# Loading k and q with three tokens side by side, and turning them two heads at a time, in a chunk-selected attention with a gated feed-forward

## The chip, the core and the metric

The kernel runs on one core of a Trainium2 chip. A core has TensorE (PE, matrix products out of the on-chip memory SBUF into the banks of PSUM), VectorE (DVE), ScalarE (ACT), GpSimd (POOL) and SyncE (SP, which issues transfers), each with its own instruction stream, and 16 DMA engines. The metric is the device time of one execution in microseconds, as the median of several runs.

## What is computed

Attention over 4 batches, 8 heads, 768 tokens and a head size of 64. Keys are cut into chunks of 32 tokens; every query keeps the six chunks with the highest upper bound of its score, and attends to the tokens of these that are not behind it. The heads side by side are the input of a feed-forward layer with a root-mean-square norm and a gate.

```python
k_min, k_max = k_chunks.min(3), k_chunks.max(3)
ub = sum(maximum(q * k_min, q * k_max), -1)          # per query and chunk, causal
top_chunks = argsort(ub)[..., -6:]
scores = q @ k.T / sqrt(64), kept where the chunk is chosen and not later
attn_out = softmax(scores) @ v
x = attn_out as (3072, 512)
xn = x / sqrt(mean(x * x) + 1e-6) * rms_g
out = (silu(xn @ w_gate) * (xn @ w_val)) @ w_out     # 512 -> 1536 -> 512
```

## The kernel before

The 32 heads are worked on as 16 pairs of heads, four pairs to a batch. Every piece of work is a step, created by a call of `add` with its name, and a long string, `PROGRAM`, writes out the order of all steps: a word such as `P155:5` means step 155, on TensorE (P), with buffer slot 5; A is ScalarE, D VectorE, G GpSimd, S SyncE. Each engine carries out its words in that order. Numbers that `add` is given as durations and loads served to find an order; they change nothing in what an engine executes.

The steps of one pair, in `prep`:

- `kload`, `qload` (lines 494 to 511): k or q of two heads come from memory as fp32 into a tile `knat` or `qnat` of 128 partitions x 6 blocks x 2 heads x 64. Token 128 t + p of a head lies in partition p, block t, so one contiguous run is one token of one head, 64 words or 256 bytes. Two transfers per tensor, one per head; for pair 0 in halves.
- `kT`, `qT` (lines 517 to 522): three blocks are turned into one PSUM bank, by three transpositions on TensorE of 128 tokens x 128 (two heads of 64) against an fp32 identity. A tensor of a pair takes two such banks. For 16 pairs these are 32 banks of k and 32 of q.
- `kE`, `qE` (lines 530 to 533): ScalarE or VectorE copies the bank, 128 x 384 words, to `kt` or `qt`.
- `kmx`, `kmn`, `dif`: minimum, maximum and difference of each chunk from `kt`. `kC`: GpSimd casts `kt` to bf16 for the scores. For q, the first three pairs (`QM = 3`) are cast from `qt` in the same way (`qC`); later pairs are cast from `qnat` as it was loaded (`qN`, then turned by a DMA, `qX`).
- `relu`, `ub`: the upper bounds are a sum of two fp32 products, of the chunk minima with q and of the differences with relu(q). For the first six pairs `bounds` at line 731 writes 2 (products) x 3 (thirds of the queries) x 2 (heads) products at line 737, for two pairs together `duo` writes 2 x 4 x 2 at line 795. Each has 64 rows and 32 columns of weights and is put at its own place of the array by `tile_position`.
- `up`, `ubm`, `max`, `sel`: transposing back, the causal mask, the six best, the choice.

Then `scores` (`sc` line 882, `exp` line 899, `av` line 918), `norm` and `ffn` (`gate` line 1051, `tanh`, `tg`, `val` line 1072, `hh`, `po` line 1092). The weights of the feed-forward are loaded in halves from GpSimd's queue (`wg`, `wv`, `wo`).

`busy` steps (line 339) are fillers on TensorE: a product of zeros with 512 columns, used by nothing. 48 may be placed; the order has 26 of them.

Of the kernel before, what the change touches and what calls it, by code (L numbers as in the profile page):

```python
# [28 lines left out]
    "S83:0 S88:1 S89 S82 D3 G0 D56 D55 D53 D54 D60 G63 A2 G65 P4:0 D59 P5:1 G66 P6:2 D58 P7:3 D57 G67 P8:4 S154:2 "  # L29
    "P9:5 G68 P86:6 S159:3 P10:7 G72 A87:0 P11:0 A69 D97:0 P92:1 D96:0 P12:2 G64 S335:4 G73 P84:3 D93:1 P90:4 A85 "  # L30
    "P13:5 P14:7 A91 P15:6 D95 P16:0 A99:0 P17:2 G101 D94 S222:5 P157:1 P155:5 D98 G62 A158:2 D103:3 P18:3 G61 "
    "P19:7 P20:4 S71 D156 P104:6,0 G102 D1 D52 D165:1 G168:1 P160:2 S330:6 A106:0 P162:3 D164:1 G74 A105 P21:1 "
    "A161:4 P107:7 A163 G167 P336:4 S70 D108:0 P338:5 A171:5 P22:0 G166 D109:2 P23:6 P24:1 A100 D110 S541:0 "
    "P172:2,3 A337:6 D112:0 A339 D111 P225:7 A173:0 D174 P113:0 G346:3 A226:1 S227:1 P175:6 A114 P223:1 D176:1 "
    "P25:4 P26:5 D177:3 P331:2 P333:3 D178 A224 G115:0 S404:2 P119:7 D332:2 A334 P147:6 A179:1 P135:4 D340:4 "
    "A148:0 G170 P128:5 P116:0 A136:1 D180 S399:3 P544:1 A117:2 D341:2 P150:3 P125:2 A545:0 P181:6 P141:4 A151:3 "
    "D232:5 A126:4 P138:0 G342 G236:2 P347:1,3 A120:5 D182 A129:6 G169 P228:2 A139:7 P230:7 S546:5 G183:1 D348:0 "
    "A349 P542:5 D229:5 A231 P350:6 D233:3 A142:8 P190:0 G345:0 P118:1 P121 A239:6 P144:3 P149:2 D351:2 P152 "
    "P184:7 G234 G235 A191:9 D352:6 P240:4,6 D543 A145:2 G238 D353 A185:5 P215:0 P122:5 G251:2 A241:0 D242 P143 "
    "A216:0 P146 P131:3 P243:7 A354 P405:4 A123:3 G237 D244:0 P209:6 P140 P137 A132:8 P218:0 D245:7 P193:7 A210:2 "  # L40
    "G358:3 P407:5 D406:3 A219:7 P203:3 A194:1 D246 P133 P124 P187:6 A408 D248:0 G247 P127 A204:8 P196:0 D153:0 "
    "P402:4 A188:3 P199:7 P217:5 P249:3 D355 A197:4 P130 P212:2 D250 S356:0 P211 A403:4 P195:6 G556:1 P206:0 "
    "A200:0 A213:6 P186 P400:4 G555:1 D134 A207:2 P264:7 P201 S357 P286:3 P214 P277:2 A265:1 G554 D401 P189 "
    "P258:0 P252:1 A278:5 D409:0 G343 P274:7 A259:0 S475:6 P261:4 A253:6 P205 D552:0 P192 G344 P198 P255:2 A275:3 "
    "P271:0 G415:1 D202 A256:8 S470:1 P267:1 P279:7 P220 P208 A287:9 A268:4 P266:2 D551:1 P283:6 A272:5 P288 "
    "P362:3 P257 P276 A262:7 P280:1 S75 D221 P269 P254 P369:0 P260 A281:2 P359:4 G412:2 D410:1 A370:1 P263 P282 "
    "A284:9 P273 P366:5 G76 D270 A363:8 P285 A360:3 P389:1 G77 P371:0 P364:6 P386:3 D329 A367:4 P361 P373:2 "
    "A390:6 G411 D365 G553 P368 P395:4 G78 A387:0 P471:5 D372 P416:7,1 D472:6 A1248:2,0 D1246:1 A1247:2 P379:6 "
    "P478:3 D418:0 A396:7 P547:0 D1249:3 D417 P27:5 A374:2 G1250:4 P397:1 D548:5 P392:4 P476:7 A380:5 P382:5 "
    "P473:2 D1251:0 A383:9 P391 P388 P376:0 A393:1 D1254:1 P375:6 P384 P1252:5 A479:2 P394 D1257:2 P381 A477 "  # L50
    "P1255:4 P419:3 A377:8 D398 G486:0 P1258:7 A1253:0 P378 D1259 P549:0 A1256 D385 P28:1 P29:5 A474 D420:1 "
    "P1260:7 A1336:5,0 D421:7 G413 P1280:1 A1335:1 D480:6 P1268:4 A1337:2 G414:0 D422 A1261:0 P1285:6 D1338:0 "
    "D423 A1281:1 D424 G1339:1 P1270:5 D1262:2 A1286:3 S426 D1282:4 P1275:2 A1271:5 D1346:3 P1263:3 A1276:6 S425 "
    "D1272:7 P1265:7 D1277:0 P1305:1 D1343:0 A1266:1 S559:0 P1288:5 D550 D1264:0 P1344:2 G557:3 P1315:0 D1287:5 "
    "A1345 S564:4 D1267:6 P439:3 A1316:2 P449:6 D1289:1 P445:2 P1300:7 A450:3 D1269:2 P1295:5 G427:0 A440:4 "
    "D481:2 A1301:3 P1283:6 A446:7 D1317:1 G79 A1296:5 P457:4 D1302:6 P560:3 A458:6 P436:2 G482 D1297:2 P1347:0 "
    "G81 A561:1 P562:7 D1348 P565:4 A563 D1284:3 P428:5 P463:3 A437:0 D1340:1 P432:0 G572:0 P487:7,6 A429:2 "
    "D570:3 A464:9 P1273:2 G451 A489:0 D488 A566:4 P1341:5 G485:0 P567:3 A1306:3 D1342 P459:6 A433:1 P490:7 "
    "D1274:4 G430 P1364:4 D569:2 G80 P466:5 P1349:0 A467:5 D491:0 P465 P442:2 D571 D568 P1399:5 A443:8 D1307:5 "
    "P460:7 P452 D575:2 A1400:4 P1278:3 A461:6 D1401:7 P577:2,1 A1350:3 D492:3 A1365:4 D493 G494 P453:7 P1308:5 "  # L60
    "A582:0 D578 A454:9 P1298:1 D1309:5 G455 P583:2 G484:2 D1299:6 P579:7 P462 D1366:5 P456 P1389:5 G434 D581:2 "
    "G483 D580:1 P468 P1392:1 D585 A1390:2 D584 D469:1 G573 P1310:4 D586:4 P1318:7 D592:5 D495 P1402:2 D1351:4 "
    "S496 P1374:6 D1279:7 D1391:3 P438:0 P1354:3 S497 D1393:8 P1303:5 D1403:9 A1355:0 P1367:1 A1375:2 D587 "
    "A1311:3 S700:3 D1319:10 P1290:2 G588 D1356:7 G498:1 P1379:7 D1312:1 A1291:0 P1293:3 D1368:11 A1380:3 G576:2 "
    "D1304:12 P524:4 P1325:1 D1292:5 A525:3 G574:0 D1294:13 P503:5 P444 D1381:6 P510:2 G526 P431 P447 P528:4 D593 "
    "A511:6 P1313:3 D589 A529:9 G594 P435 D1376:0 P703:7 S591 A504:5 P701:2 D1314:14 P1394:4 D595 D702:0 P537:6 "
    "P507:5 S590 P520:3 A538:0 D704 A1395:5 P1326 A521:8 D1396:3 P513:2 G522 S597 P1359:6 A514:2 P539:7 P441 "
    "P499:3 P1327 D448 A500:7 S596 A1360:2 P534:4 G501 P598:2 D1328:0 P1352:0 A535:1 G505 S682:1 A508:0 P516:3 "
    "P523 P506:1 D1353:15 P1384:4 A599:4 D1361:1 A517:8 P530 P536 P531:5 S705:5 D710:7 A1385:5 P512 P509 P665:0 "
    "A532:5 G714:2 P515 P678:2 P527 D1386:4 P672:3 A666:9 P518 P675:6 G558:3 D711:1 S841:2 P533 A673:1 P606:5 "  # L70
    "P502 P669:4 A679:6 P644:0 A676:0 D540 P661:3 G667 P1320:2 A607:2 G713 S823:0 D519 A662:3 P685:6 A670:8 "
    "P674:7 G663 P680 P623:5 D686:5 P657:3 P668 P683:1 G715:1 S687:6 A658:5 A645:7 P671 P1321 D684 A624:1 G646 "
    "D693:2 P648:4 G625 P651:6 S1329 P640:3 A649:6 P654:0 D692:0 P612:1 A641:9 P1322 A613:8 G642 P677 P706:5 "
    "D1323:1 G696:0 A655:0 P650:4 P842:3 S828:4 D707:3 A652:6 P647 P614:1 G712 P609:2 G600 P656 A843:4 P664 "
    "P626:0 P643 A610:7 P653 D681 G694 P633:5 S1324 P708:6 A634:8 P659 P615:3 P601 P826:2 A709 P611 P824:7 S846:3 "
    "D827:2 P602:5 G716:6 P630:6 A825 D660 P1369:2 A616:0 A603:3 D834:0 P1357:7 A631:1 S987:1 P608 A1370:2 P619:3 "
    "D833:6 P690:4 G604 A620:9 P636:5 P617 P635 G699:0 P688:6 D1371:5 A691:1 P605 P627:3 A689 P632 S982:5 D618 "
    "P844:2 G858:1 A628:6 P1362:4 D1358:16 A845 P629 A698:0 P831:6 D852:3 G621 P1382:1 A637:5 G854:1 P622 P638 "
    "P718:3,7 D639 G695 D1363:17 A1425:1,0 G697:0 P1377:2 A1426:1 D719:0 G717:2 P849:5 A1424:2 P720:0 D850:5 "
    "P1404:4 A1510:2,0 G835 D1378:18 P847:3 D721:0 A1405:2 P829:5 D832:1 A1511:1 P1330:2 D1427:3 D1406:7 G1428:4 "  # L80
    "A848 D722:1 P1407:6 A830 A723 D1429:2 P1387:4 D1433:0 P724:3 S1430:1 P1331 D1408:19 D1383:20 P1397:0 S1434 "
    "D1431:3 P1372:5 D1398:21 P1409:7 S1432 D1388:22 D1373:23 P1419:6 D726 S1105:0 D733:5 P1414:1 D734 D725 P1420 "
    "G735 D736 P1415 D851:7 S737 P1455:0 D727:0 D728 P1440:4 S738 A1456:1 D730 P1332 A729 D853 A839:0 S731 "
    "P1460:5 A1441:0 A1512:2 P1410 A1461:2 S732 A1333:2 P1445:3 D1462:7 D1442:6 P983:2 P1411 D1513:6 S969:2 "
    "A984:3 G1514:1 A1446:3 P789:5 P785:4 D1412:0 G856:1 P1421 A790:4 S1334 D1447:4 A786:7 G838:0 S1413 P792:2 "
    "D857:6 P760:7 A1422:1 P781:5 S1110:6 G855 P747:3 A793:2 P1450:4 D1457:5 A748:0 D1517:1 P753:6 A782:8 P1470:2 "
    "S964:3 A761:3 P739:0 D1519:2 P1435:3 A1471:2 G762 A740:1 D1472:0 P1108:5 S1123:4 A1436:3 P743:7 G783 P1438:0 "
    "D1109:4 A1451:1 D1437:2 A754:6 P1416 S1520 A744:9 P755:2 P1106:5 G745 D1417:2 P816:3 G741 P746 S1128:0 "
    "P795:6 D1452:3 A817:5 P791:7 P1443:1 G840:3 D1439:24 A1107 P742 P819:4 P750:3 D1444:25 S1423 P1465:0 A820:6 "
    "G787 A796:9 D1115:3 S1518 P859:5,4 A751:4 A1466:1 D1515:0 S1418 D1467:2 P967:1 S1516 A864:0 D860 P756:6 "  # L90
# [1073 lines left out]
```

## Time and profile before

| | |
|---|---|
| median of three runs | 311.89 us (311.79 to 312.59) |
| the profiled execution | 312.63 us |
| its span, first to last instruction | 310.9 us |
| TensorE busy | 300.8 us (97%) |
| VectorE, ScalarE, GpSimd busy | 232.2, 182.2, 119.5 us |
| read from memory, written | 28.57 MB, 6.29 MB |
| packets of the hardware queue q1 | 83152 |

The profile is of one execution. PE stands for products on TensorE and PEld for its weight loads, which overlap them. The ends of products are modelled, so spans of PE overlap, and what a product costs in a row of others is better read from the chain of waits, where pieces stand end to end. In groups of instructions the columns are line, engine, operation, out<-in, shape and count, then busy us and the mean of one in ns, then the idle time of the engine just before them and what ended it. "128*128" behind an operation on TensorE is the size of the array's tile in rows*columns.

### The profile page before, as it was taken

How to read it: one execution, taken by the hardware profiler on the slowest of the kernel's cores; microseconds unless marked ns; L12 is line 12 of the kernel's file. 1: busy time of each engine (PE TensorE's matmuls, PEld its weight loads, DVE VectorE, ACT ScalarE, POOL GpSimd, SP SyncE). 2: the span in 40 equal slices, each digit the busy share in tenths (PEclk: the TensorE clock that was granted, in tenths of full speed). 3: DMA queues.
4: the chain of work that ended last, by engine and by line, in shares of the span. 5: the costliest groups of instructions: out<-in, count | busy, mean ns of one | idle time of the engine just before them, and what ended most of it. 6: DMA issues, size and time to landing. Idle time of an engine off the chain costs nothing.

```text
span 310.9 us, 7415 instructions
## 1 busy us (share of the span) xinstructions
PE 300.8 (97%) x2764; PEld 190.4 (61%) x2782; DVE 232.2 (75%) x651; ACT 182.2 (59%) x405; POOL 119.5 (38%) x176
## 2 busy tenths in 40 slices
PE   7989998999999999999999999999999999999995
PEld 3657875666667764667776456666665455565542
DVE  5888988998977887789987897875743764477621
ACT  5789987672588763866997336667872303433110
POOL 8588856654547840632775104514030110000000
PEclk9999999999999999999999999999999999999999
DMA  9999999999999997996237136533000055200013
GB/s 172 221 170 175 121 209 209 158 168 150 154 176 206 201 163 145 231 163 165 55 26 50 33 74 178 53 74 29 3 0 2 34 86 186 102 2 0 0 70 136
DMA packets 113300, 35.35 MB, mean 114 GB/s; under 512 B 106224, under 2 KB 110064, under 8 KB 113264
## 3 DMA queue, kind: packets, MB, share of 16 engines
q1 hardware_dynamic: 83152, 26.62, 43.0%
q0 software_dynamic: 28512, 7.87, 25.4%
q10 hardware_dynamic: 1600, 0.39, 0.6%
q8 instruction: 22, 0.36, 0.5%
q14 instruction: 14, 0.11, 0.1%
HBM read 28.57 MB, written 6.29 MB: 112 GB/s over the span
## 4 chain that ended last, share of the span: by engine, by line
PE 87%; DMA 8%; POOL 2%; ACT 1%; issue 1%; ACTq 0%; SPq 0%; POOLq 0%
PE vp L1072 20%; PE po L1092 20%; PE gp L1051 19%; PE sc L882 10%; PE av L918 6%; DMA wg<-in_moe_w_gate_dram 5%; PE pq L520 3%; PE pk L520 3%; PE ub L795 2%; DMA knat<-in_k_dram 2%; PE ub L737 1%; DMA qnat<-in_q_dram 1%; POOL ke L294 1%; PE up L817 1%; PE busy L339 1%; POOL rt L638 1%
## 5 line engine op out<-in xcount | busy, mean ns | idle before, releaser
L899 ACT ACTIVATE pt<-sc 128x512 bf16<-128x512 f32 (+1 forms) x192 | 94.0, 556 | 21.2 <-PE sc L882 18.4
L1058 ACT ACTIVATE sg<-gp 128x384 bf16<-128x384 f32 x96 | 45.7, 495 | 72.2 <-PE gp L1051 62.6
L1072 PE MATMUL vp<-xT,wv 128*128 128x384 bf16 x384 | 74.4, 326 | 1.6 <-DMA wv<-in_moe_w_val_dram 1.5
L1051 PE MATMUL gp<-xT,wg 128*128 128x384 bf16 x384 | 74.2, 326 | 0.1
L1092 PE MATMUL po<-wo,hh 128*128 128x512 bf16 x271 | 66.8, 379 | 0.7
L1064 DVE SCALAR_TENSOR_TENSOR tg<-sg,gp 128x384 bf16<-128x384 bf16 x96 | 51.9, 549 | 20.6 <-ACT sg L1058 19.2
L1080 DVE TENSOR_TENSOR hh<-vp,tg 128x384 bf16<-128x384 f32 x96 | 51.5, 552 | 18.5 <-PE vp L1072 17.7
L882 PE MATMUL sc<-qs,ke 128*128 128x128 bf16 (+4 forms) x420 | 59.3, 251 | 0.0
L1072 PEld LDWEIGHTS <-wv 128*128 128x128 bf16 x384 | 35.8, 98 | 26.4 <-DMA wv<-in_moe_w_val_dram 1.8
L1051 PEld LDWEIGHTS <-wg 128*128 128x128 bf16 x384 | 35.7, 98 | 22.5 <-DMA wg<-in_moe_w_gate_dram 0.5
L1092 PEld LDWEIGHTS <-hh 128*128 128x128 bf16 x288 | 27.5, 98 | 27.5
L918 PEld LDWEIGHTS <-pt 128*128 128x128 bf16 x672 | 34.8, 98 | 11.1 <-POOL pt L905 0.3
L918 PE MATMUL av<-vx,pt 128*128 128x65 bf16 x672 | 41.2, 193 | 0.1
L905 POOL TENSOR_SCALAR_AFFINE_SELECT pt<-pt 128x512 bf16<-128x512 bf16 (+1 forms) x48 | 24.5, 522 | 38.5 <-ACT pt L899 38.1
L882 PEld LDWEIGHTS <-ke 89*128 89x128 bf16 (+1 forms) x420 | 31.0, 97 | 10.0 <-issue 1.4
L294 POOL CAST ke<-kt 64x768 bf16<-64x768 f32 x30 | 25.3, 846 | 7.3 <-PE sc L882 2.8
L987 POOL TENSOR_TENSOR ri<-ms,mhalf 128x3 f32<-128x3 f32 x8 | 7.2, 904 | 33.6 <-DVE ms L979 33.5
L995 DVE SCALAR_TENSOR_TENSOR xs<-xb,ri,gains 128x512 bf16<-128x512 bf16 x24 | 17.2, 751 | 3.1 <-POOL ri L987 2.9
L939 DVE TENSOR_TENSOR xb<-av,rden 128x384 bf16<-128x384 f32 (+1 forms) x34 | 18.2, 534 | 1.2
L520 PE MATMUL pk<-ident_f,knat 128*128 128x128 f32 x96 | 16.0, 282 | 1.7 <-DMA knat<-in_k_dram 1.7
L476 POOL DMA_DIRECT2D vx<-in_v_dram x16 | 17.3, 1079 | 0.1
L653 DVE MAX8 m<-ubm 128x8 f32<-128x8 f32 (+4 forms) x192 | 16.8, 160 | 0.2
(91 smaller groups left out, 300.6 us busy)
## 6 DMA issues: line engine op xcount, KB each, us to landing
out_dram<-osb SPq DMA_DIRECT2D x24, 256.0 KB, 2.3
knat<-in_k_dram SPq DMA_DIRECT2D x30, 192.0 KB, 4.4
qnat<-in_q_dram SPq DMA_DIRECT2D x30, 192.0 KB, 5.1
vx<-in_v_dram POOLq DMA_DIRECT2D x16, 192.0 KB, 5.9
wg<-in_moe_w_gate_dram POOLq DMA_DIRECT2D x2, 768.0 KB, 11.7
wv<-in_moe_w_val_dram POOLq DMA_DIRECT2D x2, 768.0 KB, 10.6
wo<-in_moe_w_out_dram POOLq DMA_DIRECT2D x2, 768.0 KB, 11.8
qs<-qn SPq DMA_TRANSPOSE x26, 2.8
```

What stands on the lines that cost most here:

```text
L294: engine[e].tensor_copy(out_, in_)
L520: nc.tensor.transpose(t[:, j * P:(j + 1) * P], nat[w].tile[:, j0 + j].rearrange("p h d -> p (h d)"), ident_f[:])
L882: nc.tensor.matmul(t[:, x:x + m, :].rearrange("p a b -> p (a b)"), ke[kk, kb * P:(kb + 1) * P], qs[kk, q0 * P:(q0 + m) * P], start=not tri ...
L899: nc.scalar.activation(out=t[:, 0:nn, :], in_=sc.tile[:, 0:nn, :], func=ACT.Exp, scale=SCALE)
L905: nc.gpsimd.affine_select(out=pt.tile[:, 0:nd, :], in_=pt.tile[:, 0:nd, :], compare_op=ALU.is_ge, fill=0.0, base=0, pattern=[[0, nd], [1, ...
L918: nc.tensor.matmul(av.tile[:, qi - i0, :], pt.tile[:, x, :], VX[c.v.slot][:, hl * NT + kb, :], start=(begin and m == 0), stop=(left[0] == ...
L1051: nc.tensor.matmul(t[:], wg[:, g, hs], XT[b].tile[:, g, cols], start=(g == 0), stop=(g == NP - 1))
L1058: nc.scalar.activation(out=t[:], in_=gp.tile[:], func=ACT.Tanh, scale=0.5)
L1064: nc.vector.scalar_tensor_tensor(out=t[:], in0=sg.tile[:], scalar=1.0, in1=gp.tile[:], op0=ALU.add, op1=ALU.mult)
L1072: nc.tensor.matmul(t[:], wv[:, g, hs], XT[b].tile[:, g, cols], start=(g == 0), stop=(g == NP - 1))
L1080: nc.vector.tensor_tensor(out=t[:], in0=vp.tile[:], in1=tg.tile[:], op=ALU.mult)
L1092: nc.tensor.matmul(po.tile[:], hhs[ht].tile[:, th * P:(th + 1) * P], wo[:, ht, :], start=(ht == 0), stop=(ht == NHT - 1))
```

## The change

**Load.** For k of all 16 pairs (`K3 = 16`) and q of the first three (`Q3 = 3`), three consecutive tokens of a head lie side by side in a partition: token 384 g + 3 p + s is in partition p, group g, place s. One contiguous run is 768 bytes. The bytes and the number of transfers stay.

**Turning.** The two heads of a token block no longer lie side by side, so a block is turned by two products with the fp32 identity, each with 64 columns of weights, head h into rows 64 h to 64 h + 63 of the bank, by `tile_position=(0, 64 h)`. A bank takes six products instead of three transpositions. This holds for 32 banks of k and 6 of q; 26 banks of q are turned as before.

**Eviction.** The bank's columns are (s, x) and the copy writes them in the order (x, s), so that `kt` and `qt` are in the order of tokens as before.

**VDIRECT**, another way to load v, is added as an empty tuple and not used.

```diff
+    K3, Q3 = 16, 3
+    VDIRECT = ()
...
+            three = p < (K3 if w == "k" else Q3)
+
+            def load(e, w=w, src=src, three=three, r0=0, rn=nb):
+                if three:
+                    if nat[w].tile is None:
+                        tile_of(nat[w], [P, NT // 3, 2, 3 * D], FP32, w + "nat")
+                    for hl in range(2):
+                        eng = nc.scalar if p == 0 and hl else nc.sync
+                        eng.dma_start(out=nat[w].tile[:, r0 // 3:(r0 + rn) // 3, hl, :],
+                                      in_=src[b, h0 + hl, r0 * P:(r0 + rn) * P].rearrange(
+                                          "(g p s) d -> p g (s d)", p=P, s=3))
+                    return
...
-                          load=3 * P * 550) for r0 in range(0, nb, 3)]
+                          load=3 * P * (380 if three else 550)) for r0 in range(0, nb, 3)]
...
+                    if three:
+                        for j in range(3):
+                            for h in range(2):
+                                nc.tensor.matmul(
+                                    t[h * D:(h + 1) * D, j * P:(j + 1) * P],
+                                    nat[w].tile[:, j0 // 3, h, j * D:(j + 1) * D], ident_f[:],
+                                    start=True, stop=True, tile_position=(0, h * D))
+                        return
...
-                tr = add(w + "T", "PE", 0.33, rank(at, b, w + "T", j0, "step"), turn, [ld[j0 // 3], c_id],
+                tr = add(w + "T", "PE", 0.83 if three else 0.33, rank(at, b, w + "T", j0, "step"), turn, [ld[j0 // 3], c_id],
...
+                    if three:
+                        evict(e, big[w].tile[:, j0 * P:(j0 + 3) * P].rearrange("p (x s) -> p s x", s=3),
+                              bank.tile[:].rearrange("p (s x) -> p s x", s=3))
+                        return
```

**Order.** `PROGRAM` is another string from its first line to its last. Its beginning:

```diff
-    "S83:0 S88:1 S89 S82 D3 G0 D56 D55 D53 D54 D60 G63 A2 G65 P4:0 D59 P5:1 G66 P6:2 D58 P7:3 D57 G67 P8:4 S154:2 "
...
+    "S82:0 S83 S88:1 S89 G0 D3 D60 P4:0 P5:1 A2 G65 D59 P6:2 P7:3 G66 D54 D57 P8:4 S154:2 D53 D55 D56 P84:5 D52 "
```

What of it matters here: it has 14 fillers instead of 26. On TensorE the 38 banks that are turned in the new way stand in 27 runs of one to four banks, three of them right behind a `ub` step. Ahead of the first `gate` step stand 16 banks of k and 15 of q (before: 14 and 14), and ahead of the first `val` step stand nine `gate` steps (before: two). GpSimd's queue issues both halves of `wg` and then both of `wv` (before: a half of each, then the second half of `wg`, the fifth load of v and the second half of `wv`). The row of gains is loaded behind k and q of pair 7 (before: behind those of pair 5).

More of the change, by code (lines that the diff above doesn't have):

```diff
@@ L473, in load_v, with get @@
         b, h0 = c.b, c.h0
+        if c.p in VDIRECT:
+            vn = Buf("nat")
+            def get(e):
+                t = tile_of(vn, [P, 2 * NT, D], FP32, "vnat")
+                nc.sync.dma_start(out=t[:], in_=v[b, h0:h0 + 2].rearrange("h (t p) d -> p (h t) d", p=P))
+            x = add("vget", "SP", 1.0, rank(lr, b, "vload"), get, opens=[vn], load=S * 550)
+            c.vload = add("vC", "", {"POOL": pool(2 * NT * D), "DVE": 0.5, "ACT": act(2 * NT * D)},
+                          rank(lr, b, "vload"), lambda e: evict(e, VX[c.v.slot][:, :, 0:D], vn.tile[:]),
+                          [x] + c_vx, opens=[c.v], uses=[vn], port=True)
+            return
         def go(e):
@@ L492, in prep @@
             nat[w], big[w] = Buf("nat"), Buf("qt")
-            def load(e, w=w, src=src, r0=0, rn=nb):
+            three = p < (K3 if w == "k" else Q3)
[9 more added lines that the diff above has]
+                    return
                 if nat[w].tile is None:
@@ L506, in prep @@
                           lambda e, load=load, r0=r0: load(e, r0=r0, rn=3), opens=[nat[w]],
-                          load=3 * P * 550) for r0 in range(0, nb, 3)]
+                          load=3 * P * (380 if three else 550)) for r0 in range(0, nb, 3)]
             else:
                 ld = [add(w + "load", "SP", 1.4, rank(lr, b, w + "load"), load, opens=[nat[w]],
-                          load=n * 550)] * 2
+                          load=n * (380 if three else 550))] * 2
             ready[w] = ld
@@ L515, in prep, with turn @@
                 bank = Buf("ps", "prep")
-                def turn(e, w=w, j0=j0, bank=bank):
+                def turn(e, w=w, j0=j0, bank=bank, three=three):
                     t = tile_of(bank, [P, 3 * P], FP32, "p" + w)
+                    if three:
[6 more added lines that the diff above has]
+                        return
                     for j in range(3):
@@ L528, in prep, with out_ @@
                     continue
-                def out_(e, w=w, j0=j0, bank=bank):
+                def out_(e, w=w, j0=j0, bank=bank, three=three):
                     if big[w].tile is None:
                         tile_of(big[w], [P, S], FP32, w + "t")
+                    if three:
+                        evict(e, big[w].tile[:, j0 * P:(j0 + 3) * P].rearrange("p (x s) -> p s x", s=3),
+                              bank.tile[:].rearrange("p (s x) -> p s x", s=3))
+                        return
                     evict(e, big[w].tile[:, j0 * P:(j0 + 3) * P], bank.tile[:])
```

245 rows, old and new, of the table PROGRAM are left out of this document.

## The prediction

> **What bounds the kernel now.** First the head of the page, for the engine that is full and for where it is not.
>
> ```profile
> span 310.9 us, 7415 instructions
> ...
> PE 300.8 (97%) x2764; PEld 190.4 (61%) x2782; DVE 232.2 (75%) x651; ACT 182.2 (59%) x405; POOL 119.5 (38%) x176
> ...
> PE   7989998999999999999999999999999999999995
> ...
> PEclk9999999999999999999999999999999999999999
> DMA  9999999999999997996237136533000055200013
> ```
>
> TensorE is busy for 97% of the span at full clock, while the transfers are dense only in the first 16 of 40 slices. A busy TensorE can still be waiting inside its modelled spans, so next the busy time in three stretches (columns: stretch, its length, then busy us and count of PE, PEld, DVE, ACT, POOL, then clock, DMA share, GB/s), and after them the same first stretch for the fillers of L339 alone (PE, PEld, clock, DMA share, GB/s).
>
> ```profile
> 0.00:57.00 57.00, 51.65 (x609) 35.46 (x611) 47.24 (x154) 45.57 (x101) 38.98 (x59) 1.00 1.22 179
> 57.00:306.00 249.00, 248.10 (x2153) 154.62 (x2168) 184.09 (x497) 136.08 (x303) 80.53 (x117) 1.00 0.58 98
> ```
> ```profile
> 0.00:57.00 57.00, 8.96 (x25) 2.84 (x26) 1.00 1.22 179
> ```
>
> From 57 us to 306 us TensorE is idle for 0.9 us in all. Whatever is added to it there is added to the end. Before 57 us it is idle for 5.35 us, and 25 recorded fillers (of the 26 in the order) run, which compute nothing. That is the only slack. What it waits for, in total, times, longest:
>
> ```profile
> PE pk L520 <- DMA knat<-in_k_dram: 1.7, 2, 1.3
> PE vp L1072 <- DMA wv<-in_moe_w_val_dram: 1.5, 1, 1.5
> PE busy L339 <- DVE zeros L334: 1.2, 1, 1.2
> PE pq L520 <- DMA qnat<-in_q_dram: 0.5, 1, 0.5
> PE pq L520 <- ACT pt L899: 0.2, 1, 0.2
> ```
>
> All late transfers together cost TensorE 1.7 + 1.5 + 0.5 = 3.7 us. So a change that trades TensorE time for transfer time starts badly: it pays in the full resource and earns in one that is waited for 3.7 us.
>
> **Part 1, the turning on TensorE.** What one bank of three token blocks costs now, and what an fp32 product in a small tile costs, can be read from the chain of waits, where pieces stand end to end (start us, us, what).
>
> ```profile
> 8.85 0.66 PE pk L520 x6
> 9.50 0.65 PE busy L339 x3
> 10.15 1.01 PE ub L737 x24
> 11.16 0.81 PE pq L520 x6
> ...
> 12.52 0.66 PE pq L520 x6
> ...
> 64.17 0.76 PE vp L1072 x4
> ...
> 68.66 0.65 PE vp L1072 x4
> 69.31 1.45 PE ub L795 x32
> ```
>
> Six transpositions take 0.66 us, 0.110 us each, so a bank of three takes 0.33 us. The bounds (L737, L795) are the only fp32 products that are not transpositions. The code of L737 gives 2 x 3 x 2 = 12 of them to a chain piece that counts 24, and that of L795 gives 2 x 4 x 2 = 16 to one that counts 32: every fp32 product runs as two records. The groups with their shapes confirm it:
>
> ```profile
> L520 PE MATMUL pk<-ident_f,knat 128*128 128x128 f32 x96 | 16.0, 282 | 1.7 <-DMA knat<-in_k_dram 1.7
> ...
> L795 PE MATMUL ub<-qt,ku 64*32 64x384 f32 x80 | 4.4, 495 | 0.0
> L795 PE MATMUL ub<-rt,ku 64*32 64x384 f32 x80 | 4.3, 482 | 0.0
> L737 PE MATMUL ub<-qt,ku 64*32 64x256 f32 x72 | 3.9, 388 | 0.0
> L737 PE MATMUL ub<-rt,ku 64*32 64x256 f32 x72 | 3.8, 376 | 0.0
> ```
>
> L737 runs 6 times (72 + 72 = 6 x 24) and a transposition is one record (96 for 32 banks of three). Tiles run side by side: L737 uses 6 tiles, so 24 records are 4 rounds; L795 uses 8, so 32 are 4 rounds. The two differ by 128 columns in each round and by 1.45 - 1.01 = 0.44 us, which is 0.110 us for a record of 128 columns, just what a transposition takes. A turning by product therefore costs two records, 0.22 us, where the transposition costs 0.110. The change needs six per bank, two heads in tiles 0 and 64 side by side: 3 x 0.22 = 0.66 us, **0.33 us more per bank**. Nothing here has a 128*64 tile, so bounds: if the second record cost nothing, 0.33 us a bank (0 more); if the two heads went one after the other, 6 x 0.22 = 1.32 us (0.99 more). I take 0.66, because the six and eight tiles of the bounds do run side by side and do take both records.
>
> There are 16 x 2 banks of k and 3 x 2 of q: 38 x 0.33 = **12.5 us**.
>
> The Trainium skill ("TensorE: Matmul & The Clock Gate", Terms) says transposing mode is 4x faster for fp32. The rows here give 2x (0.22 against 0.110). By 4x the full-width product would be 0.44 us, a bank 1.32 us and this term 38 x 0.99 = 37.6 us; that is a rival below.
>
> **Part 2, changing the tile.** The bounds also show what it costs to go into a small tile and out. Of the 1.01 us, 4 x 0.22 = 0.88 are rounds, so 0.13 are lost; and the first group behind is longer (0.76 for four vp against 0.65, so 0.11). That is 0.24 us a visit. In the new order the 38 banks stand in 27 runs; three of them stand right behind bounds, where a visit shares one side: 27 x 0.24 - 3 x 0.12 = **6.1 us**. Bounds: 0.13 a visit (3.5 us, if the work behind were late anyway) and 0.27 (7.3 us, if the 64-column weights, twice the columns of the bounds', took 0.03 more to load).
>
> **Part 3, what it frees.** Fillers fall from 26 to 14. A filler costs 0.65 / 3 = 0.216 us: 12 x 0.216 = **-2.6 us**. They stood where the order expected TensorE to wait, so this counts only if the place is filled with work: 22 of the 38 banks now stand ahead of the first gate product, 7.3 us more of it. Bounds: 0 and -5.6 us (all 26).
>
> The loads: 256 B packets become 768 B, a third in number. Now, and for the output's 2 KB packets from 300 to 311 us (queue: packets, MB, share of 16 engines):
>
> ```profile
> q1 hardware_dynamic: 83152, 26.62, 43.0%
> ```
> ```profile
> q1 hardware_dynamic: 864, 1.57, 38.3%
> ```
>
> 43.0% of 16 x 310.9 us over 83152 is 25.7 ns a packet; 38.3% of 16 x 11 us over 864 is 78 ns for 2 KB, or 29 ns for 768 B by size. One 768 B packet replaces three of 25.7 (77 ns): saved between nothing (78 against 77) and 48 ns. I take 40, as the price by size is nearest to what a longer packet costs. The loads of those 22 banks are eight of k and three of q, 512 packets each: 5632 x 40 ns / 16 = 14 us of all engines, out of 57 x 1.22. Much, but TensorE waits for transfers 3.7 us only, and the rest falls into time in which it works. The wait of the first val product (1.5) should go in any case: nine gate products now stand before it, not two, though the two halves of wg are now issued ahead of wv on POOL, so wv lands later. I take three quarters, **-2.8 us**; bounds 0 and the whole idle time, -5.35.
>
> **Part 4, edits costed at nothing.** The eviction writes every third word instead of a row:
>
> ```profile
> L290 ACT ACTIVATE kt<-pk 128x384 f32<-128x384 f32 x19 | 9.4, 497 | 3.3 <-PE pk L520 1.9 <-PE sc L882 1.2
> ...
> L294 DVE COPY kt<-pk 128x384 f32<-128x384 f32 x13 | 7.1, 550 | 2.6 <-PE pk L520 2.6
> ```
>
> No row shows this stride. Were it twice as slow, the 22 banks before 57 us would add 11 us, half to ACT and half to DVE, which have 57 - 45.57 = 11.4 and 57 - 47.24 = 9.8 us free there; without that cover it is at most 5.5 us. Work moved between ACT, DVE and POOL lies under TensorE, which is idle for 0.9 us in 249 once past 57 us. SP issues each load with the two instructions of before; k and q of a pair now follow each other sooner, and the gains row comes behind them, needed first by the norm. No wait is added to any engine; a PSUM bank is held 0.33 us longer for its turning, which is in the term of part 1. VDIRECT is empty, so v is loaded as before.
>
> **Sum.** The profiled execution lasted 312.63 us (310.9 span and 1.7 around it), 0.74 over the median of 311.89. 312.63 + 12.5 + 6.1 - 2.6 - 2.8 = 325.8, less 0.74 = **325 us**, 4.2% slower. With the bounds of parts 2 and 3: 312.63 + 12.5 + 3.5 - 2.6 - 5.35 - 0.74 = 320 at the low end, 312.63 + 12.5 + 7.3 - 0.74 = 332 at the high.
>
> **Rivals.**
> *Small tiles one after the other, or a dearer product (0.10).* With 1.32 us a bank the first term is 37.6 instead of 12.5: 350 us. For it: no row has 128 rows in a small tile. Against: the bounds' tiles overlap fully. The skill's 4x ends here as well.
> *The early stretch is paced by transfers (0.07).* If the 14 us are what holds the first 57 us, all its slack goes: 5.35 idle and 26 x 0.216 = 5.6 in fillers. 311.89 + 18.6 - 10.95 = 319.5. For it: DMA at 1.22 there. Against: only 3.7 us of waits name a transfer.
> *The turning costs what a transposition costs (0.06): not slower.* If a 128*64 product with the identity runs as one record, a bank stays at 0.33 and only the visits remain: 311.89 + 6.1 - (5.4 to 10.95), so 307 to 312.6, in the middle 310. It decides at 6.1 + 38x = 10.95, below x = 0.13 us more a bank with all slack used. Against: all bounds, by both rows, take two records.
> *Forecast (0.77).* 325 us, own range 320 to 332.
>
> **How the numbers follow.** The range 317 to 333 holds the forecast and its bounds and the rival of transfers; left out are 350 (0.10) and 310 (0.06). About 0.3% is what a measurement of this kernel can tell from no change (311.0 to 312.8). Slower: 0.77 + 0.10 + 0.07 = 0.94, less a little for a chance that the slack hides more, 0.93. The last rival lies on both sides of the band: faster 0.05, same 0.02.
>
> **What would show it.** L520 of pk with 32 x 12 = 384 records instead of 96, and of pq 96 - 18 + 72 = 150; a chain piece of a single pk bank at 0.66 us, and the next group behind it 0.1 us longer. 14 fillers. No wait of TensorE for knat or wv above 1 us. PE busy after 57 us as full as now, and some 8 us longer. q1 with 19 x 1024 = 19456 packets fewer than 83152. If pk had 192 records, or a bank took 0.33 us, the first term falls; if DMA shares fall and the time before the first val product shrinks by more than 5 us, part 3 is too small.

## The result and the profile after

The changed kernel takes 324.1 us in the median of four runs (323.59 to 324.44), against 312.14 us for the kernel before (311.79 to 312.59): 1.0381 times as long, with a 95% interval of 1.0360 to 1.0402. The forecast was 325 us. Where the runs of one kernel lie far apart (E1, E5, E11 and E12 below), those more than 1.5% above its fastest are left out of its ratio and given beside it.

The head of the page after, with the queue of the loads:

```profile
span 322.6 us, 8083 instructions
...
PE 317.0 (98%) x3112; PEld 202.0 (63%) x3112; DVE 229.5 (71%) x640; ACT 193.9 (60%) x422; POOL 112.3 (35%) x170
...
PE   8999999999999999999999999999999999999994
...
DMA  6999999999699993941470739333000045200032
...
q1 hardware_dynamic: 64720, 26.62, 36.5%
...
q10 hardware_dynamic: 576, 0.39, 0.5%
```

The span grew by 322.6 - 310.9 = 11.7 us. The hardware queue moves the same 26.62 MB in 83152 - 64720 = 18432 packets fewer. (The forecast put all of 19456 on this queue; the other 1024 went from ScalarE's queue, q10, which had 1600 before.) The busy time in stretches, same columns as before:

```profile
0.00:57.00 57.00, 55.63 (x778) 40.86 (x779) 45.41 (x145) 43.63 (x90) 36.43 (x58) 1.00 1.02 184
57.00:306.00 249.00, 249.00 (x2277) 155.44 (x2276) 179.11 (x488) 148.25 (x329) 75.92 (x112) 1.00 0.55 93
```

Ahead of 57 us TensorE is now idle for 1.37 us (before 5.35), behind it for nothing (before 0.9). The transfers' share ahead of 57 us fell from 1.22 to 1.02. And of the waits of TensorE one is left, which has nothing to do with a load:

```profile
PE busy L340 <- DVE zeros L335: 1.2, 1, 1.2
```

So the waits for loads are gone, and TensorE got longer all the same. That the wider packets took them away is not shown by this: E3 has the old packets and hardly more waits. What the turning costs stands in the chain of waits (start us, us, what):

```profile
3.56 2.79 PE pk L546 x24
6.34 1.77 PE pq L546 x24
8.11 0.32 PE busy L340
8.43 1.46 PE pk L546 x24
...
86.58 0.65 PE vp L1108 x4
87.23 0.81 PE pk L546 x12
88.03 0.32 PE sc L918
88.35 0.81 PE pk L546 x12
89.16 0.76 PE vp L1108 x4
```

A bank is 12 records, two to a product. A lone bank takes 0.81 us; two in a run take 1.46, so the second costs 0.65. The four products of `vp` behind a bank take 0.76 us, without one ahead 0.65. A bank is therefore 0.65 us, and a visit to the small tile 0.16 in the piece and 0.11 behind it at most, 0.25 us as a round figure. The groups of the turning and of its evictions:

```profile
L546 PE MATMUL pk<-ident_f,knat 128*64 128x128 f32 x384 | 27.7, 288 | 0.0
...
L291 ACT ACTIVATE kt<-pk 128x384 f32<-128x384 f32 x23 | 15.6, 702 | 9.3 <-PE pk L546 6.8 <-POOL ri L1023 1.4 <-POOL qn L295 1.0
...
L295 DVE COPY kt<-pk 128x384 f32<-128x384 f32 x9 | 6.0, 682 | 6.5 <-PE pk L546 6.5
```

The copies that write every third word take 702 ns on ScalarE (497 before) and 682 on VectorE (550 before).

### The profile page after: what moved, and what is told of

Read it like the earlier page. It is cut to its first block, busy times and chain, and to the rows that moved or that the text cites. A ratio compares the mean times of both kernels' runs of the same rounds, so it can differ in the third digit from the quotient of the medians.

```text
span 322.6 us, 8083 instructions
## 1 busy us (share of the span) xinstructions
PE 317.0 (98%) x3112; PEld 202.0 (63%) x3112; DVE 229.5 (71%) x640; ACT 193.9 (60%) x422; POOL 112.3 (35%) x170
## 3 DMA queue, kind: packets, MB, share of 16 engines
q1 hardware_dynamic: 64720, 26.62, 36.5%
## 4 chain that ended last, share of the span: by engine, by line
PE 97%; ACT 1%; issue 0%; DVE 0%; ACTq 0%
PE vp L1108 19%; PE gp L1087 19%; PE po L1128 19%; PE sc L918 12%; PE pk L546 8%; PE av L954 6%; PE pq L552 3%; PE ub L831 2%; PE ub L773 2%; PE pq L546 2%; PE busy L340 1%; PE up L853 1%; PE sc L924 1%; ACT pt L935 1%; PE up L797 1%; PE tp L1053 0%
## 5 line engine op out<-in xcount | busy, mean ns | idle before, releaser
L935 ACT ACTIVATE pt<-sc 128x512 bf16<-128x512 f32 (+3 forms) x192 | 94.8, 555 | 22.7 <-PE sc L918 18.6
L1108 PE MATMUL vp<-xT,wv 128*128 128x384 bf16 x384 | 75.7, 326 | 0.0
L1128 PE MATMUL po<-wo,hh 128*128 128x512 bf16 x288 | 69.3, 379 | 0.0
L918 PE MATMUL sc<-qs,ke 89*128 89x128 bf16 (+5 forms) x420 | 56.8, 251 | 0.1
L941 POOL TENSOR_SCALAR_AFFINE_SELECT pt<-pt 128x256 bf16<-128x256 bf16 (+1 forms) x48 | 24.9, 528 | 66.9 <-ACT pt L935 66.5
L918 PEld LDWEIGHTS <-ke 89*128 89x128 bf16 (+1 forms) x420 | 30.1, 97 | 10.8 <-issue 2.7
L295 POOL CAST ke<-kt 64x768 bf16<-64x768 f32 x32 | 26.7, 838 | 15.0 <-PE sc L918 12.3
L546 PE MATMUL pk<-ident_f,knat 128*64 128x128 f32 x384 | 27.7, 288 | 0.0
L546 PEld LDWEIGHTS pk<-ident_f,knat 128*64 128x64 f32 x384 | 21.7, 142 | 5.1 <-issue 1.4
L291 ACT ACTIVATE kt<-pk 128x384 f32<-128x384 f32 x23 | 15.6, 702 | 9.3 <-PE pk L546 6.8
L293 ACT ACTIVATE osb<-po 128x512 f32<-128x512 f32 x14 | 8.4, 609 | 18.1 <-PE po L1128 13.4
```

What stands on the lines that cost most here:

```text
L295: engine[e].tensor_copy(out_, in_)
L546: nc.tensor.matmul(t[h * D:(h + 1) * D, j * P:(j + 1) * P], nat[w].tile[:, j0 // 3, h, j * D:(j + 1) * D], ident_f[:], start=True, stop=Tr ...
L918: nc.tensor.matmul(t[:, x:x + m, :].rearrange("p a b -> p (a b)"), ke[kk, kb * P:(kb + 1) * P], qs[kk, q0 * P:(q0 + m) * P], start=not tri ...
L935: nc.scalar.activation(out=t[:, 0:nn, :], in_=sc.tile[:, 0:nn, :], func=ACT.Exp, scale=SCALE)
L941: nc.gpsimd.affine_select(out=pt.tile[:, 0:nd, :], in_=pt.tile[:, 0:nd, :], compare_op=ALU.is_ge, fill=0.0, base=0, pattern=[[0, nd], [1, ...
L1108: nc.tensor.matmul(t[:], wv[:, g, hs], XT[b].tile[:, g, cols], start=(g == 0), stop=(g == NP - 1))
```

## The experiments

All kernels of a group ran beside the kernel before on the same chip. "First group" is E1 to E4 (before: 313.12 us), second E5 to E7 (312.91), third E8 to E10 (312.98), fourth E11 and E12 (312.98).

**E1, the order alone.**

```diff
-    K3, Q3 = 16, 3
+    K3, Q3 = 0, 0
```

> The new order with the load and the turning of before (K3 = Q3 = 0). Theory (TensorE pays for the turning): the work of TensorE is that of before less 12 fillers. It loses 38 x 0.327 = 12.4 us of second records and 27 x 0.247 - 3 x 0.094 = 6.4 us of visits to the small tile against the changed kernel, and gets some waits for transfers back ahead of 57 us, at most what before had there (5.35 idle + 5.6 of fillers). Expected 310 us, between 305.5 and 314. Rival (the new order itself costs part of the 12 us): above 316 us.

Measured: 313.93 us in the median of six runs (311.69 to 315.37), ratio 1.0013 (0.9968 to 1.0058); four more lie from 318.69 to 322.01, and the median of all ten is 314.81. That is at the upper end of what was allowed for, 4 us above what was expected, and the interval includes no change, so the order alone does not cost the 12 us. But it does not win either, and single runs lie up to 10 us apart. The chain shows the start of TensorE at half pace, six transpositions in 1.51 us instead of 0.66:

```profile
4.12 4.53 DMA knat<-in_k_dram
...
8.79 1.51 PE pk L552 x6
10.30 0.85 PE busy L340 x2
11.16 0.64 PE pq L552 x3
```

**E2, the code alone.** The changed kernel with the string of the order of before.

```diff
-    "S82:0 S83 S88:1 S89 G0 D3 D60 P4:0 P5:1 A2 G65 D59 P6:2 P7:3 G66 D54 D57 P8:4 S154:2 D53 D55 D56 P84:5 D52 "
...
+    "S83:0 S88:1 S89 S82 D3 G0 D56 D55 D53 D54 D60 G63 A2 G65 P4:0 D59 P5:1 G66 P6:2 D58 P7:3 D57 G67 P8:4 S154:2 "
...
```

> The order of before with the new load and the new turning. Theory: here the 38 banks stand in 31 runs, five of them beside bounds: 12.4 + 31 x 0.247 - 5 x 0.094 = 19.6 us more on TensorE, less what ends of its waits for transfers (3.7 us at most): 312.1 + 19.6 - 3 = 329 us, between 326 and 332. Rival (the new order makes the time): within 3 us of 312. Rival (transfers pace the first 57 us): below 322.

Measured: 327.16 us (325.83 to 328.24), ratio 1.0421 (1.0353 to 1.0489). The new code makes the time, under either order; both rivals fall. Which part of the code it is, E3 and E4 separate. The new order is worth 2 to 3 us to the new code: 327.16 against 324.1, or 14.0 against 12.0 us over the kernel before that ran beside each.

**E3, the turning alone.**

```diff
-                if three:
+                if False:
                     if nat[w].tile is None:
...
-                                    nat[w].tile[:, j0 // 3, h, j * D:(j + 1) * D], ident_f[:],
+                                    nat[w].tile[:, j0 + j, h, :], ident_f[:],
...
-                    if three:
-                        evict(e, big[w].tile[:, j0 * P:(j0 + 3) * P].rearrange("p (x s) -> p s x", s=3),
-                              bank.tile[:].rearrange("p (s x) -> p s x", s=3))
-                        return
```

> The new order and the new turning by two products in small tiles, but the tokens loaded as before in packets of 256 B (and the eviction in plain order). Theory: TensorE does the same work as in the changed kernel; only waits for k and q come back (before had 1.7 + 0.5 us): 324.1 + 0 to 3, say 325.5 us. Rival (the early stretch is paced by transfers, 14 us of all engines given back): 330 us or more.

Measured: 324.59 us (324.38 to 325.23), ratio 1.0344 (1.0270 to 1.0418), against 324.1 of the changed kernel and its 1.0381. With all loads back at 256 B the time moves by 0.5 us, no more than the groups differ by. Ahead of 57 us the queue q1 carries the same bytes in both (6.95 and 6.97 MB) and takes 72.0% of the engines here and 54.3% in the changed kernel, so the wider packets free 0.177 x 57 = 10 us of all engines; the forecast said 14. They are worth next to nothing while TensorE carries this turning; the rival falls.

**E4, full width.** As E3, but one product per block:

```diff
-                            for h in range(2):
-                                nc.tensor.matmul(
-                                    t[h * D:(h + 1) * D, j * P:(j + 1) * P],
-                                    nat[w].tile[:, j0 + j, h, :], ident_f[:],
-                                    start=True, stop=True, tile_position=(0, h * D))
+                            nc.tensor.matmul(
+                                t[:, j * P:(j + 1) * P],
+                                nat[w].tile[:, j0 + j].rearrange("p h d -> p (h d)"), ident_f[:],
+                                start=True, stop=True)
```

> As the run with the turning alone, but each block is turned by one fp32 product of full width (128 columns of weights, no small tile) instead of two in small tiles. Theory: two records per product remain, 0.66 us a bank, and the visits go: 27 x 0.247 - 3 x 0.094 = 6.4 us less than the turning alone, about 319 us. Rival (the small tile is the whole price): 12.4 us less still, about 307 us. Rival (a full-width fp32 product costs four times a transposition): 1.32 us a bank, 344 us or more.

Measured: 320.02 us (319.43 to 320.47), ratio 1.0194 (1.0133 to 1.0256), 4.6 us under E3 where 6.4 were expected. Its chain:

```profile
98.70 0.67 PE pk L545 x6
99.37 0.12 PE av L949 x4
99.49 0.75 PE pk L545 x6
100.24 0.37 PE av L949 x12
```

A bank by full-width products takes 0.67 us in six records: twice a transposition, not four times, and nearly the same as the 0.65 with two small tiles side by side. So the small tile itself wins and loses next to nothing inside; going in and out is what it costs. The stretch ahead of 57 us, E3 and then E4 (columns as before):

```profile
0.00:57.00 57.00, 55.20 (x775) 40.50 (x777) 42.28 (x145) 41.55 (x90) 36.87 (x58) 1.00 1.25 186
0.00:57.00 57.00, 53.99 (x654) 42.02 (x656) 44.54 (x148) 43.13 (x95) 36.88 (x58) 1.00 1.23 188
```

Of the missing 1.8 us, 1.2 are idle time there (53.99 us busy against 55.20); another part is the 0.08 us by which some full-width banks are longer behind other work (0.75 against 0.67).

**E5, the order alone with more fillers.** Seven fillers more, as in:

```diff
-D56 P84:5 D52 
+D56 P18:1 P84:5 P19:2 P20:3 D52 
```

> The new order with the load and the turning of before, as in the run of the order alone, with seven fillers more among the first turnings of pair 0 (21 instead of 14). Theory: the order alone won nothing because its TensorE, with fewer products early, ran at half pace until 13 us (six transpositions 1.51 us instead of 0.66); the fillers keep it working while it waits for the first loads, full pace comes at about 7 us as in the kernel before, and 2 to 4 us are won: 309 to 312 us, and the spread of the runs (311.7 to 322) shrinks. Rival (the waits for transfers and for other engines set the early stretch, not the pace): 313 to 316 and the spread stays.

Measured: 322.42 us in the median of six runs (316.30 to 324.07); the two that count for the ratio are 316.30 and 319.25, ratio 1.0155 (1.0085 to 1.0225). The fillers do bring the full pace by 7 us (one takes 0.63 us at 5.91 and 0.38 at 6.94), and yet even the fastest run is above the 309 to 312 that were expected. The theory of the pace falls. The only trace is of one of the longer executions (322.91 us); its chain of waits names what held it, which says nothing of the two shorter runs:

```profile
39.53 13.88 DMA gains<-in_moe_rms_g_dram
...
53.52 0.76 DVE xs L1031
54.29 0.05 issue
54.33 0.61 PE tp L1053 x4
```

The row of gains, issued behind the loads of pair 7, landed 13.9 us later; the norm waited for it and TensorE for the norm, 6.1 us.

**E6, the first seven pairs.**

```diff
-    K3, Q3 = 16, 3
+    K3, Q3 = 7, 3
```

> The changed kernel with the new load and turning for k of the first seven pairs only (K3 = 7); k of pairs 7 to 15 as before. Theory: these 18 banks stand where TensorE is full, so their second records (18 x 0.327 = 5.9 us) and their 14 runs of visits (14 x 0.247 = 3.5 us) go in full: 324.1 - 9.4 = 314.7 us, between 313.5 and 316. Rival (the price falls early, where the loads are): above 320.

Measured: 317.66 us (316.69 to 317.99), ratio 1.0146 (1.0104 to 1.0189): 6.4 us less than the changed kernel, not 9.4. The rival falls. The waits of TensorE and its busy time in the two stretches show where the rest is:

```profile
PE sc L918 <- DMA qs<-qn: 1.8, 2, 1.6
PE busy L340 <- DVE zeros L335: 1.2, 1, 1.2
PE pk L552 <- ACT rt L672: 1.2, 1, 1.2
```
```profile
0.00:57.00 57.00, 55.46 (x770) 40.24 (x772) 45.07 (x149) 45.18 (x95) 36.48 (x58) 1.00 1.05 186
57.00:306.00 249.00, 245.10 (x2138) 152.87 (x2154) 180.59 (x491) 145.57 (x325) 75.74 (x112) 1.00 0.58 95
```

With less to do, TensorE meets work that isn't ready: it is idle for 1.5 + 3.9 us in these stretches, 4.1 more than the changed kernel, and 1.8 + 1.2 of that are waits that the changed kernel does not have. So its work fell by somewhat more than the 9.4, and 4.1 came back as idle time.

**E7, plain eviction.**

```diff
-                    if three:
-                        evict(e, big[w].tile[:, j0 * P:(j0 + 3) * P].rearrange("p (x s) -> p s x", s=3),
-                              bank.tile[:].rearrange("p (s x) -> p s x", s=3))
-                        return
```

> The changed kernel with the copies out of the banks writing whole rows, as before, so that the tokens of kt and qt stay in the order in which they were turned and another computation results; all else the same. Theory: the copies of kt become shorter (ACT 702 ns to some 500, VectorE 682 to some 550), but lie under TensorE: 324 us, within 1 us of the changed kernel. Rival (the longer copies hold up the early stretch): 321 us or less.

Measured: 323.87 us (323.71 to 323.92), 0.2 us from the changed kernel. This kernel leaves out the sorting of the tokens in the copy, and its copies of `kt` take 491 ns on ScalarE and 557 on VectorE. The longer ones lie under TensorE; the rival falls.

**E8, late banks twice.**

```diff
-                        for j in range(3):
+                        for j in list(range(3)) * (2 if p >= 7 else 1):
                             for h in range(2):
```

> The changed kernel with the 18 banks of k of pairs 7 to 15 turned twice, one turning right behind the other into the same bank, so without a further visit to the small tile. Theory: they stand where TensorE is full, so all of 18 x 6 x 0.109 = 11.8 us is added: 324.1 + 11.8 = 335.9 us, within 1 us. Rival (part of the late turning lies under something else): 333 us or less. Rival (the two heads run one after the other): 18 x 1.31 = 23.6 us more, 347 us.

Measured: 336.01 us (335.90 to 336.18), ratio 1.0712 (1.0666 to 1.0757). The added 11.9 us (11.7 by the spans, 334.3 - 322.6) are the 11.8 that were worked out:

```profile
57.00:150.00 93.00, 93.00 (x977) 61.68 (x975) 68.35 (x189) 59.49 (x132) 39.97 (x56) 1.00 0.92 149
...
L546 PE MATMUL pk<-ident_f,knat 128*64 128x128 f32 x600 | 39.5, 282 | 0.0
```

From 57 us on, what is added to TensorE is paid in full, and the two heads do run side by side. Both rivals fall.

**E9 and E10, the late banks of the kernel before** by full-width products, and by products in small tiles.

```diff
+                    if w == "k" and p >= 7:
+                        for j in range(3):
+                            nc.tensor.matmul(
+                                t[:, j * P:(j + 1) * P],
+                                nat[w].tile[:, j0 + j].rearrange("p h d -> p (h d)"), ident_f[:],
+                                start=True, stop=True)
+                        return
```

E10 has in its place the six products of E3, two to a block.

> The kernel before, in its order and with its loads, where the 18 banks of k of pairs 7 to 15 are turned by full-width fp32 products instead of transpositions. Theory: the second record alone, 18 x 0.327 = 5.9 us, all of it on a full TensorE: 5 to 6 us over the kernel before on the same chip, ratio 1.016 to 1.019. Rival (a product costs four times a transposition): 18 x 0.98 = 17.7 us over it. Rival (something hides it): less than 4.

> As the run before it, with two products in small tiles instead of one of full width. Theory: the 18 banks stand in 17 runs here, one of them ahead of bounds, so 17 x 0.247 - 0.094 = 4.1 us more than with full width, and the same work inside. Rival (small tiles cost nothing, or win by being side by side): no more than full width.

Measured: E9 322.86 us (321.83 to 323.44), ratio 1.0290 (1.0248 to 1.0331), 9.9 us over the kernel before and not 5 to 6. E10 325.41 us (324.20 to 326.12), ratio 1.0371 (1.0327 to 1.0414), 2.5 us over E9 and not 4.1. The profiled execution of E9 (323.44 us) has something that was not reckoned with. Some of its waits of TensorE and, beside them, the windows around 52 us (columns as above, the clock is the last but two):

```profile
PE vp L1079 <- DMA wv<-in_moe_w_val_dram: 2.1, 1, 2.1
...
PE sc L889 <- DVE tg L1071: 0.8, 1, 0.8
...
PE pk L521 <- DVE hh L1087: 0.7, 1, 0.7
PE sc L889 <- DMA qs<-qn: 0.6, 1, 0.6
```
```profile
48.00:52.00 4.00, 1.98 (x12) 0.90 (x10) 3.93 (x21) 3.42 (x10) 3.76 (x4) 1.00 1.16 210
52.00:56.00 4.00, 3.92 (x14) 1.93 (x15) 1.04 (x2) 0.78 (x2) 0.19 (x1) 0.57 1.25 168
```

The late `wv` made TensorE wait 2.1 us, and in the 4 us behind it the granted clock was 0.57, worth an estimated 4 x 0.43 = 1.7 us. In all, TensorE is idle for 1.9 us more than in the kernel before (321.7 - 309.8 against 310.9 - 300.8, span less busy time). So of the 10.8 us by which this span is longer, 5.9 + 1.7 + 1.9 = 9.5 have a place.

The profiled execution of E10 (324.2 us) kept its clock and was idle for 10.9 us against 11.9. It is longer than that of E9 by 0.8 us of span, so by this reckoning it has 0.8 + 1.0 + 1.7 = 3.5 us more work, near the 4.1. The other runs do not bear out the part of the clock: two of the four runs of each have a lower clock (0.995 in E9, 0.992 in E10), and among the rest (321.83 and 323.02 against 324.20 and 325.25) E10 is longer by 2.3 us. So the pair shows that the 17 visits cost something, 2.3 to 3.5 us, and not that they cost 4.1.

**E11 and E12, the gains earlier**, with the orders of E5 and of E1. `S75` is the load of the gains.

```diff
- S564:6 
+ S75 S564:6 
...
- S559:1 S75 
+ S559:1 
```

> As the run with the fillers (new order, load and turning of before, 21 fillers), with the row of gains issued ahead of q of pair 7 instead of behind k of pair 7. Theory: that run lost its time because the gains landed 13.9 us after their issue, so that the norm, and TensorE behind it, stood 6.1 us and its granted clock fell for some 4 us: without that 322.4 - 6 to 8 = 315 us or less, and the runs lie closer together. Rival (other late transfers take its place): above 318, as wide as before.

> As the run with the order alone (14 fillers), with the gains issued ahead of q of pair 7. If the late gains made the spread of that run (311.7 to 322.0), the runs now lie within 4 us, at 311 to 314, and this could be the fastest of all kernels here; if the half pace until 13 us is what costs, it is 2 to 4 us slower than the run with gains and fillers.

Measured: E11 322.02 us in the median of six runs (315.08 to 327.21; the two shortest are 315.08 and 315.26, the others 321.28 and more). E12 320.14 us (319.00 to 326.05; ratio 1.0199, 1.0167 to 1.0232, by four runs). In both profiled executions the gains landed 5.4 to 5.5 us after their issue. E11 reached the 315 that were hoped for in two runs of six and is as wide as before; E12 is above everything that was expected of it, and above E1. In the profiled execution of E11 (315.08 us) the longest wait of TensorE for a transfer is 2.4 us, for v. That of E12 is one of the two longest (324.4 us), and there k of a pair is late:

```profile
PE pk L552 <- DMA knat<-in_k_dram: 9.1, 5, 4.9
PE av L954 <- DMA vx<-in_v_dram: 1.5, 1, 1.5
PE sc L918 <- DMA qs<-qn: 1.4, 1, 1.4
```

Late transfers in another place were the rival of E11. With the loads of 256 B and the new order, TensorE waits in each of these traces for another transfer: the gains in E5, v in E11, k in E12. That this is also what sets the runs of one kernel apart is likely but not shown, since each has one trace.

## Why the prediction was right

- **TensorE is the bound and what it gets is paid.** Right, and shown by E8: 11.9 us for 11.8 added behind 57 us.
- **The second record, 12.5 us.** A bank takes 0.65 us by the chain (forecast 0.66) against 0.33, so 38 x 0.32 = 12.2. Two records to a product were read off the bounds, which have 64 rows and 32 columns; with 128 rows it is the same (384 records in 32 banks). E4 shows the price without a small tile. The Trainium skill ("TensorE: Matmul & The Clock Gate", Terms) has transposing four times faster for fp32: here it is two times, 0.67 us for six records against 0.33 for three. The rival that stood on 1.32 us a bank is out.
- **The visits, 6.1 us.** 0.25 us a visit for 0.24: 27 x 0.25 - 3 x 0.12 = 6.4. E3 less E4 shows 4.6 of it, with 1.2 more given back as idle time; E10 less E9 shows 2.3 to 3.5 where 4.1 were reckoned. That visits are paid is shown; their price is somewhere from 0.14 us (2.3 / 17) to 0.27 (0.16 + 0.11).
- **Fillers, -2.6 us.** 12 fewer, as forecast; no run takes out fillers alone.
- **Idle time, -2.8 us.** Too small; this is the term that was mis-sized. Idle time fell from 5.35 + 0.9 us to 1.37 + 0, so by 4.9. The forecast took three quarters of the waits for transfers. In fact all of these went, and waits for other engines with them. The wider packets are not needed for it: E3 has none and waits 0.4 us for a transfer; E1, which differs from E3 in the turning alone, waits 2.8 us (1.2 + 1.1 + 0.5). With the longer turning TensorE had become slower than what feeds it.
- **The sum.** 12.2 + 6.4 - 2.6 - 4.9 = 11.1 of the 11.7 by which the span grew; 0.6 have no place in it. The forecast's terms gave 13.2. That the number is off by only 0.9 us is in part luck: the idle time alone was short by 2.1, and the 0.6 and a median of before that came out 0.25 us higher made up for some of it.
- **The eviction at nothing.** The cost is not nothing, 0.2 us a copy on ScalarE and 0.13 on VectorE; that it is hidden is shown by E7.
- **The value of the load.** The rival in which transfers pace the early stretch (319.5 us) fell: E3 takes the wide packets away and loses 0.5 us. What they free was over-sized as well, 10 us of all engines and not 14 (E3). With the turning of before they might be worth more, as E1, E5, E11 and E12 wait for transfers. A load of 768 B with the cheap transposition was not tried: in the new tile the two heads of a block no longer lie side by side.
- **The order.** It was costed through its fillers and runs only. By E2 it saves 2 to 3 us under the new code, near the 2.6 of its fillers; by E1 it is worth nothing under the old one. E1 has 12.2 + 6.4 = 18.6 us less turning than the changed kernel, and its span is only 10.5 us shorter (312.1 against 322.6). 5.3 us came back as idle time (53.70 and 245.59 us busy in the two stretches, against 55.63 and 249.00). Of the other 2.8, some 2 are pieces at half pace behind 8.79 us, such as six transpositions in 1.51 us.

No version here beats the kernel before. What makes the runs of E1, E5, E11 and E12 differ by up to 12 us from one to the next stays open; the traces lead only as far as late transfers, and why a transfer of 192 to 256 KB takes 5 us in one place and 14 to 17 in another is open too.

## What to carry to other kernels

Before a layout is changed to please the transfers, ask in what unit the full engine pays for it: here wide packets that were worth 0.5 us (E3) were bought with 18.6 us of TensorE time. An fp32 transposition took half the time of an fp32 product of the same shape (0.33 against 0.67 us for three), and each excursion into the small tile cost 0.14 to 0.27 us, by the chain as much for one bank as for two, so such work belongs in few long runs. And work taken off a full engine is won only as far as its feeders keep up: E6 won 6.4 of 9.4 us, E1 10.5 of 18.6.

## What was not expected of the hardware

**The pace at the start is half, and the clock column does not show it.** In the kernel after, the first 24 records of the turning take 2.79 us and the next 24 take 1.77, where 24 take 1.46 a little later. The column of the granted clock says 1.00 there (it stands ahead of the last two):

```profile
0.00:4.00 4.00, 2.76 (x10) 1.09 (x12) 2.57 (x9) 1.34 (x2) 3.12 (x10) 1.00 0.49 136
4.00:8.00 4.00, 4.00 (x46) 3.87 (x43) 1.73 (x3) 1.73 (x4) 2.69 (x9) 1.00 0.89 248
```

In E1, which has gaps between its first products, the half pace lasts beyond 11 us (two fillers in 0.85 us at 10.3), while the same column shows 1.00. The Trainium skill ("TensorE: Matmul & The Clock Gate", Part 1: The HAM clock gate) says that the array starts at half rate and needs some 3.4 us of sustained work to leave it; the trace agrees with the half rate. It lasts longer here than 3.4 us: products run without a gap from 1.24 us, and the piece that starts at 6.34 is still slow. E1 fits the word sustained, and so does E5, whose seven fillers bring the full pace by 7 us; whether the gaps matter or the kind of work in them, no run separates.

**A wait of 2 us can cost as much again.** In the profiled execution of E9 the clock fell to 0.57 for the 4 us behind a 2.1 us wait, and in that of E5 to 0.66 and 0.50 in the two stretches of 4 us from 50 us on, during and behind a wait of 6.1. In the kernel before, a wait of 1.5 us at the place of E9's left it at 1.00. So a late transfer can be dearer than its wait; from which length on, these traces do not show.

**A copy with a step of three words on its output is slower:** 702 against 497 ns on ScalarE, 682 against 550 on VectorE, for 384 words a partition. With rows written whole again (E7) they take 491 and 557.
